# Another issue order and other buffer numbers for a gated linear attention with a mixer behind it, on one core

## The chip, the core and the metric

The kernel runs on one core of one Trainium2 chip. A core has a matrix engine (TensorE, PE in the profile), three engines for elementwise work (VectorE, DVE; ScalarE, ACT; GpSimd, POOL), a fifth that here only issues transfers (SyncE, SP), and DMA engines that move data between memory and the core's buffers and can transpose a block on the way. Each engine runs its own instructions in program order, and waits on semaphores for what the others produce. The metric is the device time of one execution in microseconds. Inputs and output are float32 in memory; the products run in bfloat16 with float32 sums.

## The reference, cut to what matters

Four batches, eight heads, 768 positions, 48 channels a head. First a linear attention whose state decays by its own factor `alpha` for every channel and position; then an MLP mixer over the result, once across the positions and once across the 384 channels.

```
def _attn_ref(q, k, v, alpha):                       # each (4, 8, 768, 48)
    for t in range(S):
        state = alpha[:, :, t, :, None] * state + np.einsum('bhd,bhe->bhde', k[:, :, t], v[:, :, t])
        y[:, :, t] = np.einsum('bhd,bhde->bhe', q[:, :, t], state)

def _moe_ref(x, w_tok1, w_tok2, w_ch1, w_ch2):       # x: (4, 768, 384)
    h = np.maximum(x.transpose(0, 2, 1) @ w_tok1, 0.0) @ w_tok2      # 768 -> 256 -> 768
    u = x + h.transpose(0, 2, 1)
    return u + np.maximum(u @ w_ch1, 0.0) @ w_ch2                    # 384 -> 1536 -> 384
```

## The kernel before

**The attention** goes in 12 chunks of 256 positions, three to a batch; a number at the end of a name is the chunk. A chunk loads alpha, k, q and v (`ld_at`, `ld_kt`, `ld_qt`, `ld_vt`, each 384 KB, all issued by SP). ACT takes logarithms of alpha (`ln`, or `ln1` and `lnP` of products `P` of two neighbours), PE sums them along the positions (`cum`, `cumw` in chunks 0 to 2), ACT makes exponentials of the sums (`E` and `IE`), and `kk` and `qq` multiply k and q with them into pkk and pkq. Both are transposed into tpk and tpq: in chunks 0 to 5 by PE (`trk`, `trq`) with a copy out of the matrix engine's buffer (`evk`, `evq`), in chunks 6 to 11 by a transposing DMA that SP issues (`dk`, `dq`), with a last rearrangement `pq` of q. PE forms the products of q and k inside the chunk (`G0_`, `G1_`), DVE masks them into gtm (`mask0_`, `mask1_`, 128x1024 each). `vb` casts v, `vs0_`, `vs1_`, `ka`, `kb` and `kc` are copies that bring k and v into the form for `K`, the update of the state; `s` and `sa` with `sm` add and scale the state; `ia`, `ib` and `y0_`, `y1_` are the two parts of the output, which `x0_` and `x1_` bring out as the mixer's input.

**The mixer** goes batch by batch. `t1` and `t2` with `ht` between are the mixing across positions, `u` the addition. The transpose of u into ut is done on PE in batch 0 (`up`, `ut`) and by two transposing DMAs in batches 1 to 3 (`ux`). Then come `c1_b_mc_half` (12 column blocks of the channel layer by two halves of the positions, three matmuls of 384 columns each), its relu `rt`, `c2_b_i_q` (four groups of three matmuls for each of six row blocks), the last addition `o` and the store `st`. Weights come in 16 loads `ldw` and 16 casts `cw`. `f...` are matmuls on data that nobody reads, put ahead of a named operation.

**What sets the order.** There is no scheduler left in the file. Every operation is made as an object with its engine's alternatives, its inputs and its buffers, and a table `ORDER` names all of them in one row; the last letter of an entry is the engine (t PE, s ACT, v DVE, g POOL, y SP). They are issued in that order, so the table sets the order on each engine and, where an operation can run on two or three, which. A second table `BUFS` gives each value its buffer or bank: 21 input buffers, 8 banks of the matrix engine, 23 buffers for relu outputs and so on, taken in the order of first use. A third, `GATES`, is empty. `Plan.run` reads them:

```
out = [by[n] for n, _ in order]
for o, (_, e) in zip(out, order):
    o.on, o.gate = ENGINES[e], by.get(gates.get(o.name))
    for v in o.vals:
        if v.buf is None:
            v.buf = next(bufs)
```

One more rule ties engines together: where DVE and POOL (and their operations marked `port`) follow each other in the table, `shared` adds a dependency from the last one of the other engine, so that the two never run such operations at once. The transfers of SP share a few semaphores in turn, so that a transfer is issued when an earlier one that used the same semaphore has landed. Whatever engine issues an operation, it waits for the values that it reads and for the last reader of the buffer that it overwrites. So a load that stands behind a transposition in SP's row waits until that transposition's input is there.

Of the kernel before, what the change touches and what calls it, by code (L numbers as in the profile page):

```python
# [420 lines left out]
ld_vt2y vb2s vs1_2g vs0_2s G1_2t x0_1s K2t t1_0_0_0t t1_0_0_1t ib1t y1_1t ldw_wt11y cw_wt11s ldw_wt21y t1_0_0_2t
t1_0_1_0t t1_0_1_1t ia2t y0_2t t1_0_1_2t sa0_2v sm0_2g ib2t mask1_2v y1_2t x1_1s t1_0_0_3t t1_0_1_3t x0_2s t1_0_0_4t
t1_0_1_4t x1_2s t1_0_1_5t ht_0_1v ld_at4y P4g ldw_wt20y cw_wt20g t1_0_0_5t ht_0_0s f2_t2_0_2t t2_0_2t ln14s u_0_2v
cw_wt21g t2_0_1t u_0_1v t2_0_5t t2_0_3t u_0_3v t2_0_0t r14s ld_at3y ld_kt3y ln13s P3g t2_0_4t lnP4s cum4t lnP3s
up_0_1t ut_0_1s cum3t IE3s u_0_0v up_0_0t u_0_4v u_0_5v up_0_2t ldw_wc12y cw_wc12g ut_0_0v c1_0_4_0t c1_0_5_0t r13s
k0a3g kk3v trk3t ldw_wc10y kb3g cw_wc10s c1_0_0_0t ldw_wc13y cw_wc13s rt_0_4_0v ut_0_2v rt_0_5_0v rt_0_0_0v c1_0_1_0t
ld_qt3y E3s c1_0_1_1t c1_0_5_1t rt_0_1_0v q0r3g qq3v evk3s IE4s ka3v kc3v ldw_wc14y cw_wc14s ldw_wc15y cw_wc15g
rt_0_1_1s c1_0_0_1t rt_0_0_1s c1_0_6_0t trq3t c1_0_7_0t rt_0_6_0s ld_qt4y c1_0_4_1t q0r4g rt_0_7_0v E4s qq4g ldw_wc11y
rt_0_4_1s rt_0_5_1v c1_0_11_0t rt_0_11_0s c1_0_8_0t rt_0_8_0s cw_wc11s ld_vt3y vb3g vs0_3g c1_0_9_0t c1_0_10_1t
rt_0_9_0s evq3v G1_3t mask1_3v G0_3t mask0_3v c1_0_9_1t rt_0_10_1s c1_0_2_1t rt_0_2_1s ld_kt4y k0a4g kk4g vs1_3s  # L430
rt_0_9_1s c1_0_11_1t c1_0_8_1t rt_0_8_1s rt_0_11_1s c1_0_3_0t rt_0_3_0v trq4t evq4s ldw_wc20y ld_at5y ln15s K3t s0_3v
P5g c1_0_2_0t rt_0_2_0v sa1_3v c1_0_10_0t rt_0_10_0v c1_0_3_1t c1_0_7_1t trk4t rt_0_3_1s kb4s rt_0_7_1v evk4v
ldw_wc21y cw_wc21g ldw_wc22y ld_kt5y lnP5s c1_0_6_1t rt_0_6_1v cw_wc20s ld_vt4y ib3t y1_3t x1_3s G0_4t cum5t G1_4t
mask0_4v E5s y0_3t sm1_3g IE5s c2_0_4_0t mask1_4v x0_3v ka4g kc4g k0a5g kk5v c2_0_5_0t c2_0_3_0t c2_0_0_0t ld_qt5y
cw_wc22s c2_0_3_1t r15s q0r5v c2_0_0_1t c2_0_4_1t vb4s vs0_4s vs1_4s ia4t qq5v y0_4t x0_4s K4t sa0_4v trk5t trq5t
c2_0_5_1t ldw_wc23y ldw_wc24y ldw_wc25y cw_wc24v cw_wc23s c2_0_0_2t c2_0_5_2t evq5v sm0_4g sa1_4v sm1_4v c2_0_4_2t
evk5s G1_5t mask1_5v G0_5t cw_wc25s c2_0_5_3t o_0_5v c2_0_3_2t c2_0_3_3t o_0_3v c2_0_4_3t kc5s ld_vt5y vb5g vs0_5s K5t
sa0_5v ld_at6y ib4t y1_4t P6g lnP6s c2_0_0_3t t1_1_0_0t t1_1_0_1t t1_1_1_0t t1_1_1_1t t1_1_1_2t ia5t x1_4s t1_1_1_3t
sm0_5g mask0_5v y0_5t ib5t vs1_5v y1_5t cum6t t1_1_0_2t t1_1_0_3t ln16s x0_5s t1_1_1_4t ld_at8y ld_kt6y P8v lnP8s
t1_1_0_4t x1_5v t1_1_0_5t IE6s t1_1_1_5t ht_1_1s E6s k0a6g kk6g r16s kb6s ka6g ld_qt6y c2_0_2_0t c2_0_2_1t ld_at7y P7g  # L440
ln17s r17s lnP7s o_0_0v ht_1_0v ld_kt7y ld_vt6y o_0_4v t2_1_2t u_1_2v dk6y c2_0_1_0t t2_1_0t u_1_0v t2_1_1t u_1_1v
ux_1_0y t2_1_3t u_1_3v t2_1_5t u_1_5v q0r6g vb6g t2_1_4t u_1_4v cum8t IE8s c2_0_1_1t c2_0_1_2t E8s c2_0_1_3t o_0_1v
cum7t c2_0_2_2t c2_0_2_3t o_0_2v IE7s c1_1_10_0t c1_1_11_0t c1_1_3_0t rt_1_3_0s rt_1_11_0v c1_1_5_0t ln18s rt_1_5_0s
c1_1_8_0t qq6v k0a7g kk7v ux_1_1y c1_1_6_1t E7s rt_1_6_1s vs1_6v rt_1_8_0v c1_1_11_1t c1_1_1_0t c1_1_4_0t rt_1_4_0s
c1_1_2_0t c1_1_0_1t c1_1_10_1t c1_1_3_1t rt_1_10_1s rt_1_3_1s ld_at10y ld_qt7y kc6g q0r7g rt_1_1_0v rt_1_0_1v
c1_1_0_0t c1_1_8_1t c1_1_9_0t rt_1_2_0v rt_1_0_0s rt_1_11_1s r18s qq7g c1_1_7_1t rt_1_10_0v ld_qt8y ld_at9y rt_1_8_1s
c1_1_1_1t rt_1_1_1v c1_1_5_1t rt_1_5_1v dq6y rt_1_7_1v c1_1_4_1t rt_1_4_1v c1_1_6_0t ld_kt8y vs0_6g K6t c2_1_2_0t
s0_6v sa1_6v c1_1_7_0t c2_1_2_1t q0r8g qq8g pq6s G1_6t mask1_6v k0a8g kk8g rt_1_9_0s P10g G0_6t mask0_6v rt_1_6_0s
rt_1_7_0s c1_1_2_1t c1_1_9_1t c2_1_2_2t dq7y dk7y ln19s c2_1_2_3t pq7s o_1_2v G1_7t mask1_7v P9v ka7s kc7g rt_1_2_1s
G0_7t mask0_7v ld_vt7y c2_1_1_0t c2_1_1_1t c2_1_1_2t sm1_6g ld_vt8y vb8g dq8y ib6t c2_1_0_0t y1_6t x1_6v c2_1_0_1t  # L450
c2_1_1_3t o_1_1v vb7s vs0_7s vs1_7s kb7s K7t sa0_7v ln110s c2_1_0_2t rt_1_9_1s sm0_7v sa1_7v dk8y pq8s y0_6t ia7t
y0_7t ld_kt9y c2_1_3_0t c2_1_3_1t G0_8t r110s vs0_8g kc8g G1_8t mask0_8v c2_1_3_2t c2_1_3_3t x0_6s r19s x0_7s lnP9s
o_1_3v cum9t vs1_8s sm1_7g K8t sa0_8v c2_1_0_3t t1_2_1_0t t1_2_1_1t ib7t sm0_8g y1_7t x1_7s t1_2_0_0t ld_kt10y ld_qt9y
ld_at11y k0a10g t1_2_1_2t ia8t mask1_8v y0_8t t1_2_0_1t x0_8s ib8t y1_8t o_1_0v x1_8v t1_2_1_3t ld_vt9y ld_qt10y
t1_2_0_2t t1_2_0_3t t1_2_0_4t t1_2_1_4t t1_2_0_5t P11g ht_2_0s lnP11s E9s t1_2_1_5t ht_2_1v c2_1_5_0t c2_1_5_1t lnP10s
t2_2_4t t2_2_3t q0r9v qq9g t2_2_0t t2_2_5t t2_2_2t ld_kt11y u_2_4v u_2_3v u_2_5v cum11t E11s IE9s t2_2_1t u_2_2v
u_2_1v c2_1_5_2t IE11s c2_1_4_0t q0r10g c2_1_5_3t u_2_0v cum10t IE10s E10s c2_1_4_1t ux_2_1y c2_1_4_2t c2_1_4_3t
c1_2_9_1t k0a9g kk9v ka9v c1_2_7_1t qq10g o_1_4v rt_2_7_1v o_1_5v c1_2_10_1t c1_2_8_1t rt_2_8_1s dq9y pq9g k0a11g
kk10g c1_2_11_1t rt_2_11_1v rt_2_10_1v ln111s c1_2_6_1t rt_2_6_1s ux_2_0y c1_2_1_0t c1_2_10_0t rt_2_10_0s rt_2_9_1v
c1_2_8_0t c1_2_3_0t c1_2_5_1t rt_2_5_1v rt_2_8_0s st_1_0y dk9y kc9s G0_9t mask0_9v G1_9t rt_2_3_0s kk11v mask1_9v  # L460
# [523 lines left out]
```

## Time and profile before

| what | us |
|---|---|
| runs | 161.72, 162.14, 161.7 |
| median of the runs | 161.72 |
| the profiled execution's own time | 162.03 |
| its span, first to last instruction | 160.3 |

The profile is of one execution, on the core's own clock from the first instruction of the span. The difference of 1.7 us between its time and its span lies before and behind. The page gives each engine's busy time, and groups of instructions by source line with their mean duration in nanoseconds; a row of the stages (windows) gives, after the stretch, its length, then the busy time and number of instructions of PE, PE's weight loads (PEld), DVE, ACT, POOL and SP, then the granted clock of PE as a share of full speed, the busy share of the DMA engines and what they moved in GB/s. The chain of waits lists what ended last at each moment, followed back from the last instruction: start, length, engine and line. A row of a timeline is start, length, engine, line, operation, output and inputs, and in square brackets the idle time in front of it and what ended it. A row of the DMA list has the number of issues and the median time from the issue to the landing.

PE is the engine with the most work, 152.1 of 160.3 us. DVE has 115.0, ACT 99.1, POOL 75.9.

### The profile page before, as it was taken

What the parts mean: (1) busy time and instruction counts of PE and PEld (TensorE: products, weight loads), DVE (VectorE), ACT (ScalarE), POOL (GpSimd) and SP (SyncE); (2) the same over time, 40 slices, a digit from 0 to 9 for tenths busy, and PEclk for the clock granted to TensorE, in tenths of its full rate; (3) what the DMA queues carried; (4) which work ended last, traced back from release to release, by engine and by line L of the source; (5) the groups of instructions that cost most, each with busy time, mean ns of one, the idle gap of its engine ahead of it and who ended that gap; (6) DMA issues with size and microseconds to landing.
All of it is one profiled execution on the core that took longest, in us unless ns stands there. A gap on an engine that the chain in (4) does not pass through costs nothing.

```text
span 160.3 us, 3961 instructions
## 1 busy us (share of the span) xinstructions
PE 152.1 (95%) x1555; PEld 96.6 (60%) x1555; DVE 115.0 (72%) x205; ACT 99.1 (62%) x183; POOL 75.9 (47%) x91
## 2 busy tenths in 40 slices
...
GB/s 120 325 325 330 364 338 304 352 313 294 335 210 352 252 305 125 207 252 221 218 216 175 325 309 76 216 236 188 276 149 0 4 76 247 70 98 4 222 195 123
DMA packets 77922, 35.05 MB, mean 219 GB/s; under 512 B 70352, under 2 KB 77136, under 8 KB 77904
## 3 DMA queue, kind: packets, MB, share of 16 engines
...
q8 instruction: 12, 0.20, 0.5%
q14 instruction: 6, 0.05, 0.1%
...
## 4 chain that ended last, share of the span: by engine, by line
PE 75%; ACT 7%; DMA 6%; DVE 6%; issue 3%; POOL 1%; SPq 1%; DVEq 0%; POOLq 0%
PE ps L920 29%; PE ps L925 25%; PE ps L661 9%; PE ps L896 5%; PE ps L901 4%; DMA in<-in_alpha_dram 3%; DMA in<-in_v_dram 3%; PE ps L730 2%; ACT vb L763 2%; DVE u L905 2%; DVE pkq L718 1%; DVE pkk L718 1%; ACT tpq L763 1%; ACT x L763 1%; DVE tmp L859 1%
## 5 line engine op out<-in xcount | busy, mean ns | idle before, releaser
L925 PE MATMUL ps<-wc,rt 128*128 128x384 bf16 (+1 forms) x300 | 53.2, 319 | 0.0
L920 PE MATMUL ps<-ut,wc 128*128 128x384 bf16 x288 | 49.6, 326 | 0.1
L891 ACT ACTIVATE rt<-ps 128x384 bf16<-128x384 f32 x55 | 25.4, 490 | 25.2 <-PE ps L920 20.2
L920 PEld LDWEIGHTS <-wc 128*128 128x128 bf16 x288 | 27.5, 98 | 17.8 <-DMA ut<-u 0.3
L925 PEld LDWEIGHTS <-rt 128*128 128x128 bf16 x300 | 27.4, 97 | 15.8
L893 DVE TENSOR_SCALAR rt<-ps 128x384 bf16<-128x384 f32 x41 | 21.2, 553 | 13.6 <-PE ps L920 13.0
L788 DVE TENSOR_TENSOR gtm<-ps,mk 128x1024 bf16<-128x1024 f32 x24 | 28.7, 1218 | 3.2 <-PE ps L661 2.7
L929 DVE TENSOR_TENSOR rt<-ps,u 128x384 f32<-128x384 f32 (+1 forms) x25 | 13.4, 538 | 9.9 <-PE ps L925 9.6
L862 POOL TENSOR_TENSOR ss<-tmp,E 128x384 bf16<-128x384 f32 x12 | 10.0, 836 | 15.0 <-DVE tmp L859 9.6
L718 POOL TENSOR_TENSOR pkq<-in,E 128x768 bf16<-128x768 f32 x7 | 12.7, 1815 | 6.7 <-DVE pkq L718 3.4
L763 ACT CAST x<-ps 128x384 bf16<-128x384 f32 x17 | 8.1, 477 | 11.8 <-PE ps L661 11.8
L905 DVE TENSOR_TENSOR u<-ps,x 128x384 bf16<-128x384 f32 x24 | 11.7, 551 | 4.4 <-PE ps L901 4.1
L763 ACT CAST vb<-in 64x384 bf16<-64x384 f32 (+1 forms) x19 | 11.6, 612 | 2.7 <-DMA in<-in_v_dram 1.3
L718 DVE TENSOR_TENSOR pkk<-in,in 128x768 bf16<-128x768 f32 x8 | 7.7, 956 | 6.3 <-ACT in L705 4.3
L710 POOL TENSOR_TENSOR in<-in,in 128x384 f32<-128x384 f32 x9 | 9.0, 1002 | 5.1 <-DVE pkq L718 3.8
L764 POOL CAST vb<-in 64x384 bf16<-64x384 f32 (+1 forms) x13 | 8.5, 650 | 5.2 <-DVE ss L862 2.8
L896 PE MATMUL ps<-x,wt 128*128 128x384 bf16 x48 | 10.5, 325 | 0.0
L661 PE MATMUL ps<-rt 128*128 128x512 bf16 (+1 forms) x21 | 8.9, 528 | 1.1 <-DVE rt L547 1.1
L859 DVE TENSOR_TENSOR tmp<-ps,ss 128x384 f32<-128x384 f32 x16 | 8.8, 552 | 0.8 <-PE ps L661 0.4
L901 PE MATMUL ps<-ht,wt 128*128 128x384 bf16 x48 | 8.9, 326 | 0.1
L661 PE MATMUL ps<-tpq,tpk 48*64 48x128 bf16 (+1 forms) x288 | 8.4, 218 | 0.7 <-ACT tpq L763 0.5
L661 PE MATMUL ps<-vb,gtm 128*128 128x48 bf16 x192 | 8.7, 183 | 0.3 <-DVE gtm L788 0.3
...
## 6 DMA issues: line engine op xcount, KB each, us to landing
...
```

Source lines behind the costliest of these rows:

```text
L661: return self.pe.matmul(out, lhsT=lhsT, rhs=rhs, start=start, stop=stop, skip_group_check=True)
L718: self.shared(self.eng[e].tensor_tensor(self.t(dst)[:, :, h0:h1, 0:D], self.t(src)[:, h0:h1].rearrange("p h s d -> p s h d"), bass.AP(tens ...
L763: return self.act.copy(d, s)
L788: self.nc.vector.tensor_tensor(self.t(gtm)[:, hf, :, :], self.pair(gp).rearrange("p a (j t) -> p (a j) t", t=128), bass.AP(tensor=m.tensor ...
L891: self.act.activation(d, s, AF.Relu)
L893: self.nc.vector.tensor_scalar_max(d, s, 0.0)
L896: self.pe.matmul(self.bank(bank)[:, 0:HD], lhsT=self.wt1[:, kc, m * 128 : m * 128 + 128], rhs=self.t(x), start=(kc == 0), stop=(kc == NS - 1))
L901: self.pe.matmul(self.bank(bank)[:, 0:HD], lhsT=self.wt2[:, i // 3, kc, i % 3 * 128 : i % 3 * 128 + 128], rhs=self.t(hts[kc]), start=(kc = ...
L905: self.nc.vector.tensor_tensor(self.t(u)[:, i % 3], self.bank(bank)[:, 0:HD], self.t(x), ALU.add)
L920: self.pe.matmul(self.bank(bank)[:, 0:HD], lhsT=self.wc1[:, kc, mc * 128 : mc * 128 + 128], rhs=self.t(ut)[:, 3 * half : 3 * half + 3, kc, ...
L925: self.pe.matmul(self.bank(bank)[:, 0 : cz - ca], lhsT=self.t(rts[mc][0])[:, i * 128 : i * 128 + 128], rhs=self.wc2[:, mc, ca:cz], start=( ...
L929: self.nc.vector.tensor_tensor(self.o(o, i, ca, cz), self.bank(bank)[:, 0 : cz - ca], self.t(u)[:, i % 3, ca:cz], ALU.add)
```

## The change

Only the two tables are replaced. Every operation stays as it was, the same matmuls, relus, masks, loads and transpositions; 934 entries become 937, since the matmuls on unread data are put ahead of other operations (f8, f1, f2, f4, f1, f2, f4, f1, f2, f2, f1, f1 in place of f12, f2, f2, f1, f1, f3, f1, f2, f2). 144 operations change their engine (relus, copies, casts and products that two or three engines can do, and 11 stores), in both directions: ACT has 199 entries in place of 194, DVE 181 in place of 182, POOL 78 in place of 79, SP 92 in place of 95 (three stores go to ACT). In the shared turn of DVE and POOL, hand-overs from one to the other fall from 31 to 21. `ORDER` is one line longer, so that every line behind it has a number higher by one. The first lines of the diff:

```diff
 ORDER = """
-ld_kt0y ld_at0y ld_at1y ln0s f12_cumw0t f2_cumw0t cumw0t ld_at2y ln1s cumw1t IE0s kk0v f2_trk0t trk0t E0s ld_qt0y qq0v
-trq0t ln2s cumw2t evk0v ka0g kb0v kc0v E1s ld_vt0y vb0s vs1_0v vs0_0v f1_K0t K0t IE1s ld_kt1y kk1v E2s evq0s ld_qt1y
...
+ld_at0y ld_at1y ln0s f8_cumw0t f1_cumw0t cumw0t ln1s cumw1t ld_kt0y IE0s ld_qt0y E0s kk0v qq0v IE1s f2_trk0t trk0t
+evk0v trq0t evq0v f4_G0_0t f1_G0_0t G0_0t mask0_0v ld_qt1y E1s ka0s ld_vt0y vb0s kc0s kb0g qq1g trq1t ld_at2y ln2s
...
```

How rows move is shown at three places.

**The start, on ACT.** `la` are the logarithms of chunks 0, 1 and again 0 for chunk 2 (two buffers), `in` out of `ps` is IE, `E` is E, `vb` the cast of v, `tpq` out of `ps` is evq, `kt` and `pkk` out of `pkk` are the copies ka and kc. The order before:

```order
L655 ACTIVATE la_0_85<-in_1_65 128x16x48
L655 ACTIVATE la_1_86<-in_3_67 128x16x48
L705 ACTIVATE in_2_66<-ps_63 128x768
L701 ACTIVATE E_0_89<-ps_63 128x800
L655 ACTIVATE la_0_85<-in_6_70 128x16x48
L701 ACTIVATE E_1_90<-ps_63 128x800
L763 CAST vb_0_98<-in_1_65 128x768
L705 ACTIVATE in_4_68<-ps_63 128x768
L701 ACTIVATE E_2_91<-ps_63 128x800
L763 COPY tpq_0_105<-ps_63 128x2x512
L705 ACTIVATE in_6_70<-ps_63 128x768
```
And of the change, the same stretch:

```order
L656 ACTIVATE la_0_85<-in_0_64 128x16x48
L656 ACTIVATE la_1_86<-in_2_66 128x16x48
L706 ACTIVATE in_1_65<-ps_63 128x768
L702 ACTIVATE E_0_89<-ps_63 128x800
L706 ACTIVATE in_0_64<-ps_63 128x768
L702 ACTIVATE E_1_90<-ps_63 128x800
L764 COPY kt_0_97<-pkk_0_94 64x8x48
L764 CAST vb_0_98<-in_7_71 128x768
L764 COPY pkk_0_94<-pkk_0_94 64x8x48
L656 ACTIVATE la_0_85<-in_6_70 128x16x48
L764 COPY tpq_1_106<-ps_63 128x2x512
L706 ACTIVATE in_6_70<-ps_63 128x768
```
The logarithm of chunk 2 (the third `la` row) has gone from the fifth place to the tenth, behind ka0, vb0 and kc0 (`kt`, `vb`, `pkk`), two of which DVE or POOL did before; IE1 stands ahead of E1 in the fifth place, where it stood behind vb0; and evq1 is the only evq left in the stretch, since evq0 goes to DVE.

**SP's row from the transposition of batch 1's u on.** `ut<-u` are the two halves ux_1_0 and ux_1_1, `tpk<-pkq` the transpositions of q (dq6, dq7, dq8), `tpk<-pkk` that of k (dk7). Before:

```order
L747 DMA_TRANSPOSE ut_132<-u_130 128x9x128
L600 DMA in_82<-in_alpha_dram 128x8x96
L600 DMA in_77<-in_q_dram 128x8x96
L600 DMA in_70<-in_q_dram 128x8x96
L600 DMA in_73<-in_alpha_dram 128x8x96
L743 DMA_TRANSPOSE tpk_104<-pkq_92 128x8x128
L600 DMA in_67<-in_k_dram 128x8x96
L743 DMA_TRANSPOSE tpk_102<-pkq_93 128x8x128
L743 DMA_TRANSPOSE tpk_101<-pkk_95 128x8x128
L600 DMA in_72<-in_v_dram 128x8x96
L600 DMA in_79<-in_v_dram 128x8x96
L743 DMA_TRANSPOSE tpk_104<-pkq_92 128x8x128
```
And of the change:

```order
L748 DMA_TRANSPOSE ut_132<-u_130 128x9x128
L601 DMA in_72<-in_v_dram 128x8x96
L601 DMA in_74<-in_q_dram 128x8x96
L744 DMA_TRANSPOSE tpk_104<-pkq_92 128x8x128
L601 DMA in_73<-in_q_dram 128x8x96
L601 DMA in_70<-in_k_dram 128x8x96
L601 DMA in_65<-in_v_dram 128x8x96
L744 DMA_TRANSPOSE tpk_102<-pkq_93 128x8x128
L601 DMA in_77<-in_alpha_dram 128x8x96
L744 DMA_TRANSPOSE tpk_101<-pkk_95 128x8x128
```
The load of v of chunk 7, which stood in the tenth place behind dq6, dq7 and dk7, stands in the second directly behind ux_1_1; v of chunk 8 stands ahead of dq7, where it stood behind dk7; the loads of alpha of chunks 10 and 9 have left the place in front of dq6, one for later and one for a place behind dq7.

**DVE's row around chunk 10.** `gtm` are masks (here of chunk 9), `pkk` is kk, `pkq` is qq, `rt` with two operands is a relu, `rt` with `u` the last addition o, `ss` and `tmp` state additions. Before:

```order
L893 TENSOR_SCALAR rt_135<-ps 128x384
L788 TENSOR_TENSOR gtm_108<-ps,mk 128x1024
L718 TENSOR_TENSOR pkk_96<-in_78,in_81 128x16x48
L788 TENSOR_TENSOR gtm_108<-ps,mk 128x1024
L893 TENSOR_SCALAR rt_135<-ps 128x384
L893 TENSOR_SCALAR rt_151<-ps 128x384
L893 TENSOR_SCALAR rt_154<-ps 128x384
L893 TENSOR_SCALAR rt_144<-ps 128x384
L893 TENSOR_SCALAR rt_143<-ps 128x384
L855 TENSOR_TENSOR ss_114<-ps,E_89 128x384
L859 TENSOR_TENSOR tmp_109<-ps,ss_114 128x384
L893 TENSOR_SCALAR rt_134<-ps 128x384
```
And of the change:

```order
L894 TENSOR_SCALAR rt_135<-ps 128x384
L789 TENSOR_TENSOR gtm_108<-ps,mk 128x1024
L894 TENSOR_SCALAR rt_151<-ps 128x384
L789 TENSOR_TENSOR gtm_108<-ps,mk 128x1024
L894 TENSOR_SCALAR rt_154<-ps 128x384
L719 TENSOR_TENSOR pkk_96<-in_84,in_82 128x16x48
L894 TENSOR_SCALAR rt_153<-ps 128x384
L719 TENSOR_TENSOR pkq_93<-in_78,E_90 128x16x48
L894 TENSOR_SCALAR rt_155<-ps 128x384
L856 TENSOR_TENSOR ss_111<-ps,E_89 128x384
L860 TENSOR_TENSOR tmp_109<-ps,ss_111 128x384
L930 TENSOR_TENSOR rt_133<-ps,u_127 128x384
```
Before, kk11 stands between the two masks of chunk 9 and kk10 runs on POOL; now kk10 stands behind the second mask and a relu, with qq11 one relu behind it, and the state additions of chunk 9 (`ss`, `tmp`) behind those. The transposition dk10 on SP waits for kk10, and G0 and G1 of chunk 10 on PE wait for dk10.

127 lines of the change are left out of this document (64 added, 63 removed), and 22 rows, old and new, of the table BUFS.

## The prediction

> **What bounds the kernel now.** I read the page's busy times first, then the busy time by stages, then the chain of waits.
>
> ```profile
> PE 152.1 (95%) x1555; PEld 96.6 (60%) x1555; DVE 115.0 (72%) x205; ACT 99.1 (62%) x183; POOL 75.9 (47%) x91
> ...
> 0.00:30.84 30.84, 26.36 (x302) 15.77 (x303) 22.81 (x54) 24.05 (x37) 16.06 (x29) 1.00 1.04 305
> 30.84:85.00 54.16, 54.16 (x557) 35.21 (x558) 46.02 (x73) 42.20 (x81) 35.18 (x37) 1.00 0.99 256
> 85.00:92.00 7.00, 6.52 (x103) 4.35 (x99) 5.41 (x10) 5.62 (x11) 3.35 (x5) 1.00 1.23 251
> 117.00:157.20 40.20, 40.14 (x348) 25.58 (x346) 21.02 (x39) 10.59 (x21) 1.83 (x3) 1.00 0.31 103
> 157.20:160.40 3.20, 0.00 (x0) 0.00 (x0) 0.34 (x1) 0.00 (x0) 0.00 (x0) 1.00 0.40 146
> ```
>
> The second number of a stage row is PE's busy time. From 30.84 us to 157.2 PE is never idle but for 0.48 us between 85 and 92. A busy row can hide gaps, so I look at the pitch of the matmuls in the chain:
>
> ```profile
> 30.84 1.14 PE ps L920 x6
> 67.32 10.24 PE ps L920 x63
> 133.66 9.80 PE ps L920 x60
> ```
>
> 10.24/63 and 9.80/60 are 163 ns a matmul of 384 columns, early and late. So in this middle PE issues one matmul behind the other, and no order can shorten it except by taking out waits. (The Trainium skill, Perfetto Trace Analysis, section Identifying the Most-Contended Engine, calls matmul busy time a poor measure of headroom and would look at the LDWEIGHTS share; that is 60% here, and by it some 60 us could be won. The equal pitch speaks against it, and the sum goes by the pitch.) The span is then three pieces: the time until the first channel matmul (30.84), PE's work after it with its waits, and a tail of 3.1 us behind the last matmul. An order can change the first, the waits of the second, how much work is done before 30.84, and a little of the third.
>
> **The waits that the old order has.** PE's timeline and the chain around its only idle time:
>
> ```profile
> 87.30 1.14 PE L925 MATMUL ps<-wc,rt 128*128 128x384 bf16 x6
> 88.69 0.64 PE L661 MATMUL ps<-tpq,tpk 48*64 48x128 bf16 x32 [0.25 <-ACT tpq L763]
> 89.26 1.15 PE L925 MATMUL ps<-wc,rt 128*128 128x384 bf16 x6
> 90.64 0.32 PE L661 MATMUL ps<-la,u 128*128 128x384 bf16 x1 [0.23 <-ACT la L652]
> ...
> 78.89 0.04 SPq L743
> 78.98 4.49 DMA in<-in_v_dram
> 83.49 0.84 ACT vb L763
> 88.50 0.52 ACT lf L658
> 90.17 0.43 ACT la L652
> ...
> 77.69 1.24 SPq L743 DMA_TRANSPOSE tpk<-pkk  x1
> 80.35 3.12 SPq L743 DMA_TRANSPOSE tpk<-pkq  x1
> 87.28 1.35 ACT L763 COPY tpq<-tpk 128x1024 bf16<-128x1024 bf16 x1 [0.44 <-DMA tpk<-pkq]
> ```
>
> Six matmuls from 87.30 are through at 87.30 + 6 x 0.163 = 88.28, and G of chunk 8 begins at 88.69: 0.41 late. In the same way 89.26 + 0.98 = 90.24 against 90.64: 0.40 late. The chain says why: v of chunk 7 is asked for at 78.98, behind a transposition on SP, lands 4.49 later, and ACT is pushed back from 83.49 to 90.6 (vb, its halves, pq8, the logs, lnP9). The new order asks for v of chunk 7 directly after the second transposition of batch 1's u, ahead of dq6, and for v of chunk 8 ahead of dq7. **Term a:** both waits go, -0.8. Bounds: 0 (another input of G0_8 or cum9 is as late) and -0.81.
>
> **The start.** PE's, DVE's and ACT's timelines in the first 25 us (start, length, instruction, and in brackets the idle time before it with what ended it):
>
> ```profile
> 6.41 0.65 PE L661 MATMUL ps<-la,u 128*128 128x384 bf16 x3 [0.26 <-ACT la L655]
> 8.34 0.96 DVE L718 TENSOR_TENSOR pkk<-in,in 128x768 bf16<-128x768 f32 x1 [4.27 <-ACT in L705]
> 10.37 0.84 ACT L763 CAST vb<-in 128x768 bf16<-128x768 f32 x1
> 5.52 0.84 ACT L655 ACTIVATE la<-in 128x768 bf16<-128x768 f32 x1 [3.44 <-DMA in<-in_alpha_dram]
> 6.71 0.84 ACT L655 ACTIVATE la<-in 128x768 bf16<-128x768 f32 x1 [0.35 <-DMA in<-in_alpha_dram]
> 7.50 0.81 ACT L705 ACTIVATE in<-ps 128x768 f32<-128x768 f32 x1
> 11.80 0.85 ACT L701 ACTIVATE E<-ps 128x800 f32<-128x800 f32 x1
> 14.72 1.32 ACT L763 COPY tpq<-ps 128x1024 bf16<-128x1024 bf16 x1 [0.20 <-PE ps L730]
> 16.06 1.04 ACT L763 COPY kt<-pkk 64x384 bf16<-64x384 bf16 x2
> 19.62 1.01 ACT L763 COPY tpk<-ps 128x1024 bf16<-128x1024 bf16 x1
> 17.76 0.96 DVE L718 TENSOR_TENSOR pkk<-in,in 128x768 bf16<-128x768 f32 x1
> 19.77 0.55 DVE L859 TENSOR_TENSOR tmp<-ps,ss 128x384 f32<-128x384 f32 x1
> 23.43 1.22 DVE L788 TENSOR_TENSOR gtm<-ps,mk 128x1024 bf16<-128x1024 f32 x1
> 14.39 0.68 DVE L764 COPY tpk<-ps 128x1024 bf16<-128x1024 bf16 x1
> ```
>
> Two loads that follow each other land 6.71 - 5.52 = 1.19 apart. The first two alphas move from places 2 and 3 of SP's queue to 1 and 2, so ln0, ln1 and IE0 come 1.2 us earlier, and k of chunk 0, now third, lands when the second alpha did: kk0 starts near 7.2, not 8.34. But the third alpha falls from place 4 to 7 and lands near 6.7 + 4 x 1.2 = 11.5, and ACT then has in one row vb0 0.84, kc0 0.51, ln2 0.84, evq1 1.32, IE2 0.81, E2 0.85, evk1 1.01 = 6.2, less some 0.1 of overlap each, from vb0's load at 10.4 on: 16.1. Behind it stands G0_1, as late as it was before the change. The lead is kept on DVE alone, which has masked one more G by then. Before, DVE ran without a gap from 17.76 to 24.65 (one kk of 0.96, four masks of 1.22, three additions of 0.55, a little overlapped). Now it has one kk and one mask less, and an evk (0.68) and an x (0.48, L763 on ACT takes as long) more, but the evk waits for kk2, which went to POOL: qq2 and kk2 there are 1.8 each from about 16.05, the transposes end near 20.3, then 0.68 + 0.55 + 1.22 + 0.55 + 1.22 less overlaps is 24.3. Against 24.65 that is 0.3 earlier; two weight casts placed ahead of ht0 and among the t2 take some of it. **Term b:** -0.2; bounds -1.1 (all of the lead kept) and +0.3.
>
> POOL's 1.8 and the rest of the durations by group:
>
> ```profile
> L718 POOL TENSOR_TENSOR pkk<-in,in 128x768 bf16<-128x768 f32 x4 | 7.3, 1821 | 0.2
> tpk<-pkk SPq DMA_TRANSPOSE x6, 3.8
> ut<-u SPq DMA_TRANSPOSE x6, 2.9
> 31.97 0.45 PE ps L730 x8
> 90.93 0.33 PE L661 MATMUL ps<-vb,pkk 128*128 128x96 bf16 x4
> ```
>
> **Term c:** the eight transposes trk3 (0.45) now stand ahead of the first channel matmul, and cum4 stands behind it (a cum takes 90.93 - 90.64 = 0.29): -0.15. Fill matmuls lie before the first channel matmul in both orders and are inside term b.
>
> **Term d, the tail.** In the old order the last two additions stand apart; now o_3_4 (0.55, as a u or tmp row) ends about when the last half matmul does and o_3_0h0 follows at once: +0.05, bounds 0 and +0.2 (two stores closer together).
>
> **Term e, new waits.** The tightest place is chunk 10. DVE has, from the end of G0_9 on, mask0_9 1.22, a relu, mask1_9 1.22, a relu, kk10 0.96; with 0.55 a relu and 0.09 of overlap each that is 4.05, and 0.45 for G0_9 itself and the hand-over. Then dk10 is issued and must land before G1_10. PE has between G0_9 and G1_10 fourteen groups of three matmuls (0.49), K9 and G0_9 itself (0.33 each): 7.5. So dk10 has 7.5 - 4.5 = 3.0 us. The transposes of u, which have no load in front of them, take 2.9; those of pkk 3.8 in the median, with loads in front. Ahead of dk10 no load is issued for some 6 us, so I take the 2.9 and the wait at 0.2; bounds 0 and 0.8. Besides, G0_5 waits for evq5: trq5 (0.45 and its end) and 1.32 on ACT against 0.45 + 3 x 0.49 of PE, 0.1 to 0.2. **Term e:** +0.4, bounds 0 and +1.9.
>
> **Sum** against the profiled execution: 160.3 - 0.8 - 0.2 - 0.15 + 0.05 + 0.4 = 159.6, 0.7 less. That execution took 162.03, 1.7 outside its span; the median of the runs is 161.72, so 161.72 - 0.7 = 161.0; as the tight places can only add, I say 161.1.
>
> **Rivals.**
> 1. **The wait moves.** Term a is won, but dk10 takes the 3.8 of the median row against the 3.0 that it has: PE waits 0.8 at G1_10 in place of 0.2, 161.1 + 0.6 = 161.7, no change. For it: the median of six such transpositions; against: no load in front of this one.
> 2. **Slower: dk10 behind traffic.** dq8 was issued at 80.35 and its reader on ACT, idle until then, started at 87.28, so a transposition has taken up to 6.9 here. If dk10 takes 4.9 or more, PE stands 1.9 at G1_10 in place of 0.2, and nothing behind it gives that back, since K10, sa, sm, K11, the masks, t1_3 and the last mixer follow one from the other: 161.1 + 1.7 = 162.8. It decides from a landing 4.2 us after the issue on. For it: two of three kinds of transposition have medians of 3.8 and more; against: these lay behind two or three loads, dk10 lies behind another transposition alone.
> 3. **Head of the line on ACT.** vb7 now stands ahead of four relus. v of chunk 7 is issued 0.5 us before the batch's first channel matmul, and c1_1_3_0, eleven groups (5.4) later, needs the bank that the first of them empties; 5.4 + 0.5 - 0.84 - 0.6 leaves the load 4.4. The old one took 4.49, behind a transposition; at 5.5 PE loses 1.1: 162.2. Little chance alone; it is counted with rival 2.
> 4. **Better than forecast.** The new waits stay hidden and half of the start's lead is kept: 161.1 - 0.4 - 0.4 = 160.3.
> 5. **A slow start.** cumw0 would come at 5.2 in place of 6.41, with 8 + 1 fills before it in place of 12 + 2. The 0.65 that three matmuls take at 6.41 is the pace of the rows at 90 us (0.32 for one, 0.16 for each further one); at half that pace, an assumption, cumw0 and cumw1 take 1 us more, of which vb0's wait for its load hides 0.5: 161.6. The granted clock is 1.00 in every stage shown above, and no row here shows a slow start. (The Trainium skill, TensorE: Matmul & The Clock Gate, section Part 1: The HAM clock gate, says that the pace of the array follows its activity over a window of some 3.4 us that runs freely, so fewer fills could leave it slow in some runs; no run here shows it.)
>
> **How the numbers follow.** The forecast has 0.46, rival 1 0.16, rivals 2 and 3 0.15, rival 4 0.16, rival 5 0.07. What a measurement of this kernel can tell from no change is about 0.3%, 0.49 us: faster is below 161.23, slower above 162.21. The forecast's own range is 160.6 to 161.6, of which a fifth lies in the band; so faster is 0.36 + 0.16 = 0.52; same is 0.10 + 0.12 (rival 1) + 0.04 (rival 5) = 0.26; slower 0.15 + 0.04 + 0.03 = 0.22. The range goes from rival 4 to between rivals 3 and 2: 160.2 to 162.5.
>
> **What would show it.** Right: no idle time of PE between 85 and 92, the first channel matmul at 30.6, the last matmul's end near 156.3, DVE's last mask of chunk 2 ending near 24.3. Wrong: idle time of PE at the G of chunk 10 or 11, put down to the DMA of tpk or to ACT; an ACT wait for in_v_dram near 68 to 72 with PE waiting for rt behind it; a first channel matmul later than 30.84; or waits of 0.4 on PE at places that this text does not name, which would mean that the tightness lies in the banks and not in the transfers.

## The result, and the profile after

| | kernel before | new kernel |
|---|---|---|
| median, first comparison | 162.16 (22 runs) | 163.38 (22 runs) |
| ratio, 95% interval | | 1.0074 (1.0052 to 1.0095) |
| median, second comparison | 161.68 (35 runs) | 163.46 (12 runs) |
| ratio, 95% interval | | 1.0101 (1.0079 to 1.0123) |
| span of the profiled execution | 160.3 | 161.9 |
| first channel matmul | 30.84 | 30.53 |
| end of the last matmul | 157.14 | 158.55 |

The new kernel is slower by 0.7 to 1.0%, 1.2 to 1.8 us; the forecast was 161.1, faster, with a range of 160.2 to 162.5, and both medians lie above that range. The forecast started from a median of 161.72 in three executions; in the first comparison the kernel before has 162.16, so against a change of -0.6 the runs have +1.2. The ratios and their intervals leave out the few executions in which the chip was slower as a whole, and are not the quotients of the medians shown. The stages of the new kernel first, columns as in the prediction (length, then busy time and instructions of PE, weight loads, DVE, ACT and POOL, granted clock, DMA share, GB/s):

```profile
30.53:85.00 54.47, 53.83 (x553) 34.38 (x554) 43.25 (x69) 44.70 (x84) 39.89 (x39) 1.00 0.98 254
85.00:119.00 34.00, 32.41 (x356) 20.57 (x354) 28.17 (x47) 22.25 (x44) 15.31 (x18) 1.00 0.99 221
119.00:158.55 39.55, 39.55 (x347) 25.37 (x345) 20.30 (x37) 10.00 (x21) 2.72 (x4) 1.00 0.29 96
```

PE stands idle for 0.64 us before 85 and for 1.59 between 85 and 119; before, it was 0.48 between 85 and 92 and none in the stage ahead of that. The line of the page that gives the chain of waits by engine, of the kernel before and of the new one:

```profile
PE 75%; ACT 7%; DMA 6%; DVE 6%; issue 3%; POOL 1%; SPq 1%; DVEq 0%; POOLq 0%
```

```profile
PE 64%; DMA 15%; POOL 6%; DVE 5%; ACT 4%; issue 3%; SPq 2%; POOLq 0%; DVEq 0%
```

What PE lost in the chain went to the DMA engines (9 points) and to POOL (5). PE's timeline of the new kernel at the only three places after 31 us where the view shows a wait:

```profile
82.67 0.64 PE L662 MATMUL ps<-tpq,tpk 48*64 48x128 bf16 x32 [0.64 <-DMA tpk<-pkk]
108.58 0.98 PE L662 MATMUL ps<-tpq,tpk 48*64 48x128 bf16 x32 [0.91 <-ACT tpq L764]
117.38 0.64 PE L662 MATMUL ps<-tpq,tpk 48*64 48x128 bf16 x32 [0.55 <-DMA tpk<-pkk]
```

These are G of chunks 7, 9 and 10, and the chain (start, length) says what they waited for:

```profile
77.29 5.33 DMA tpk<-pkk
...
101.05 6.11 DMA tpk<-pkq
107.17 0.02 issue
107.19 1.34 ACT tpq L764
...
113.83 3.50 DMA tpk<-pkk
```

All three are transposing DMAs: dk7, dq9 (with pq9 behind it on ACT) and dk10. SP's timeline shows what was issued just ahead of the first two:

```profile
76.67 0.58 SPq L601 DMA_DIRECT2D in<-in_alpha_dram  x1
77.29 2.12 SPq L744 DMA_TRANSPOSE tpk<-pkk  x1
...
99.74 0.58 SPq L601 DMA_DIRECT2D in<-in_q_dram  x1
100.37 0.57 SPq L643 DMA_DIRECT2D out_dram<-rt  x1
101.05 2.02 SPq L744 DMA_TRANSPOSE tpk<-pkq  x1
```

Ahead of dk7 stands the load of alpha of chunk 9; ahead of dq9 the load of q of chunk 10 and a store. In the kernel before, SP's timeline has only a transposition directly ahead of each:

```profile
75.83 1.75 SPq L743 DMA_TRANSPOSE tpk<-pkq  x1
77.69 1.24 SPq L743 DMA_TRANSPOSE tpk<-pkk  x1
...
97.80 1.29 SPq L747 DMA_TRANSPOSE ut<-u  x1
99.19 1.25 SPq L743 DMA_TRANSPOSE tpk<-pkq  x1
```

There dk7 landed 3.10 us after its issue and dq9 2.73.

**Where the 1.5 us between the two spans went.** For each group of matmuls of one operation I take the time from its start to the start of the next, less the median of its kind in the kernel before; so a group's usual pitch counts as nothing. Between the first channel matmul and the end, the surplus is 1.53 us before and 3.40 after. The new kernel has 0.71 at G0_7, 1.20 at G1_9 and G0_9, 0.62 at G1_10, in sum 2.53. The kernel before has 0.32 at G0_8, 0.40 at cum9, 0.12 at G1_10, in sum 0.84. So the difference is made of: start -0.31, work that now lies ahead of the first channel matmul -0.16 (sum of the medians 124.37 and 124.21), old waits -0.84, new waits +2.53, tail +0.12 (3.18 and 3.30), and 0.18 spread over places of less than 0.1 each. The sum is +1.52; the spans, 160.32 and 161.85, differ by 1.53.

### The profile page after: what moved, and what is told of

The parts are those of the page before. It is cut to its first block, busy times and chain, and to the rows that moved or that the text cites. A ratio compares the mean times of both kernels' runs of the same rounds, so it can differ in the third digit from the quotient of the medians.

```text
span 161.9 us, 3944 instructions
## 1 busy us (share of the span) xinstructions
PE 152.8 (94%) x1559; PEld 95.7 (59%) x1559; DVE 115.5 (71%) x204; ACT 101.2 (63%) x185; POOL 77.4 (48%) x90
## 3 DMA queue, kind: packets, MB, share of 16 engines
q10 hardware_dynamic: 2160, 2.85, 4.8%
## 4 chain that ended last, share of the span: by engine, by line
PE 64%; DMA 15%; POOL 6%; DVE 5%; ACT 4%; issue 3%; SPq 2%; POOLq 0%; DVEq 0%
PE ps L926 25%; PE ps L921 17%; PE ps L662 10%; DMA tpk<-pkk 5%; PE ps L897 5%; PE ps L902 4%; DMA tpk<-pkq 4%; DMA in<-in_q_dram 3%; DMA in<-in_alpha_dram 3%; PE ps L731 2%; POOL pkq L719 2%; DVE pkk L719 1%; POOL pkk L719 1%; SPq L601 1%; POOL in L715 1%
## 5 line engine op out<-in xcount | busy, mean ns | idle before, releaser
L926 PE MATMUL ps<-wc,rt 128*128 128x384 bf16 (+1 forms) x300 | 51.9, 320 | 0.0
L892 ACT ACTIVATE rt<-ps 128x384 bf16<-128x384 f32 x48 | 21.8, 489 | 18.7 <-PE ps L921 9.6
L894 DVE TENSOR_SCALAR rt<-ps 128x384 bf16<-128x384 f32 x48 | 24.9, 552 | 11.6 <-PE ps L921 11.5
L764 ACT CAST vb<-in 64x384 bf16<-64x384 f32 (+1 forms) x23 | 14.0, 608 | 2.7 <-DMA in<-in_v_dram 1.5
L719 POOL TENSOR_TENSOR pkq<-in,E 128x768 bf16<-128x768 f32 x8 | 14.5, 1817 | 0.4
L719 POOL TENSOR_TENSOR pkk<-in,in 128x768 bf16<-128x768 f32 x6 | 10.9, 1816 | 5.0 <-ACT in L698 2.5
L765 POOL CAST vb<-in 64x384 bf16<-64x384 f32 (+1 forms) x10 | 6.3, 630 | 9.6 <-DVE pkk L719 5.3
L647 POOL TENSOR_TENSOR in<-in 128x384 f32<-128x384 f32 x9 | 8.9, 999 | 3.1 <-DVE in L711 3.0
L662 PEld LDWEIGHTS <-tpk 48*64 48x64 bf16 (+1 forms) x288 | 5.8, 102 | 7.5 <-DMA tpk<-pkk 2.6
L715 POOL TENSOR_TENSOR in<-in,lf 128x384 f32<-128x384 f32 x8 | 7.9, 997 | 3.3 <-ACT lf L659 2.7
```

The lines of the kernel that those rows point to most:

```text
L662: return self.pe.matmul(out, lhsT=lhsT, rhs=rhs, start=start, stop=stop, skip_group_check=True)
L719: self.shared(self.eng[e].tensor_tensor(self.t(dst)[:, :, h0:h1, 0:D], self.t(src)[:, h0:h1].rearrange("p h s d -> p s h d"), bass.AP(tens ...
L764: return self.act.copy(d, s)
L892: self.act.activation(d, s, AF.Relu)
L894: self.nc.vector.tensor_scalar_max(d, s, 0.0)
L926: self.pe.matmul(self.bank(bank)[:, 0 : cz - ca], lhsT=self.t(rts[mc][0])[:, i * 128 : i * 128 + 128], rhs=self.wc2[:, mc, ca:cz], start=( ...
```

## The experiments

Theories at the start. **Q**: a transposition lands only after the loads asked for just ahead of it, and the new order puts such loads ahead of dk7 and dq9. **L**: the transpositions are late because of late inputs or traffic at that moment, whatever stands ahead. **M**: waits only move, so one taken away comes back at the next place. The pieces of the table that move are shown; the buffers stay each operation's own, and the table of their numbers is written anew in the order of first use.

**late_at9**, one load moved.

```diff
-y1_6t kb7g ld_at9y dk7y c1_1_5_1t
+y1_6t kb7g dk7y c1_1_5_1t
...
-dk8y kc8s ld_at11y
+dk8y ld_at9y kc8s ld_at11y
```

> The new kernel with one load moved: alpha of chunk 9 is asked for behind dk8 instead of directly ahead of dk7. Theory Q (a transposition lands only after the loads asked for just ahead of it on SP): dk7 lands 2.7 to 3.2 us after its issue in place of 5.33, the wait of 0.71 at G0_7 goes, 163.4 - 0.7 = 162.7. Rival L (the transpositions are late because of the traffic or of late inputs at that moment, whatever stands ahead): dk7 still takes 5 us, 163.4. Rival M (a wait taken away comes back at the next one): the wait at G0_7 goes, that at G1_9 grows by 0.7, 163.4.

dk7 landed 2.96 us after its issue, and the wait at G0_7 went. PE's waits in the new kernel and in this one (us in total, times, longest):

```profile
PE ps L662 <- DMA tpk<-pkk: 1.2, 2, 0.6
PE ps L662 <- ACT tpq L764: 0.9, 1, 0.9
```

```profile
PE ps L662 <- ACT tpq L764: 0.9, 1, 0.9
PE ps L662 <- DMA tpk<-pkk: 0.6, 1, 0.6
```

One of the two DMA waits is gone, the others have not grown: against L and, here, against M. The median was 163.04, where 162.7 was expected. Its ratio to the kernel before, 1.0086 (1.0056 to 1.0116), lies between the new kernel's two ratios, so the trace shows this gain and the times do not; the run new_again below shows why a part of this wait is not always there.

**late_qt10_st02**, the load of q of chunk 10 and the store moved behind dk9, with q0r10, which reads that q.

```diff
-rt_2_9_1s ld_qt10y c1_2_3_0t
+rt_2_9_1s c1_2_3_0t
...
-q0r11g q0r10g c1_2_4_1t
+q0r11g c1_2_4_1t
...
-rt_2_7_1s st_0_2y dq9y pq9s rt_2_0_0s rt_2_4_1s kb9s dk9y
+rt_2_7_1s dq9y pq9s rt_2_0_0s rt_2_4_1s kb9s dk9y ld_qt10y q0r10g st_0_2y
```

> The new kernel with the load of q of chunk 10 and the store st_0_2 moved from ahead of dq9 to behind dk9 (and q0r10, which reads that q, behind them in the table). Theory Q: dq9 lands some 2.8 us after its issue in place of 6.12, the waits of 1.2 at G1_9 and G0_9 go, 163.4 - 1.2 = 162.2; G0_7 still waits 0.7. Rival L: dq9 still takes 5 to 6 us, 163.4. Rival M: the wait at G1_9 goes and that at G1_10 grows by as much, 163.4.

dq9 took 4.21 in place of 6.11 (2.8 was expected), and the waits at G1_9 and G0_9 went. But G1_10 now waits 1.06 in place of 0.62, though dk10 lands fast, as the chain shows:

```profile
111.02 2.73 DMA tpk<-pkq
114.26 2.71 DMA tpk<-pkk
```

q of chunk 10 landed at 108.03 in place of 104.14, so q0r10, qq10, k0a10 and kk10 followed later on POOL and DVE, and dk10 was issued at 114.26. Median 163.1, 1.0084 (1.0057 to 1.0112): what a wait gives, the next row takes, a part of M.

**all_three**, both moves, and mask1_9 behind kk10 on DVE.

```diff
-c1_2_9_0t rt_2_9_0v mask1_9v c1_2_5_0t
+c1_2_9_0t rt_2_9_0v c1_2_5_0t
...
-k0a10g kk10v c2_2_1_0t
+k0a10g kk10v mask1_9v c2_2_1_0t
```

> The new kernel with both moves, and with mask1_9 on DVE behind kk10, so that dk10 is issued 1.0 us earlier. Theory Q: the three waits of 2.5 us in all go, 160.9, which is 0.8% below the kernel before. Rival L: 163.4, or 162.8 with only dk10 earlier. Rival M: 162.5 to 163.4, with waits at places that had none.

165.5, 1.0225 (1.0183 to 1.0267): far off. DVE's timeline:

```profile
110.58 0.56 DVE L894 TENSOR_SCALAR rt<-ps 128x384 bf16<-128x384 f32 x1 [0.84 <-PE ps L921]
112.74 0.96 DVE L719 TENSOR_TENSOR pkk<-in,in 128x768 bf16<-128x768 f32 x1 [1.60 <-POOL in L711]
113.61 1.22 DVE L789 TENSOR_TENSOR gtm<-ps,mk 128x1024 bf16<-128x1024 f32 x1
```

kk10 waits 1.60 for POOL's k0a10, and everything behind it on DVE waits too: the mask, and the relus whose banks PE needs. PE then stood 2.56 us longer than usual before K9 and 0.3 to 0.5 at each of four groups after it. The third part of this edit, the mask behind kk10, cost more than the two moves won: two_moves below, without it, takes 162.76. In the trace of late_qt10_st02, too, kk10 waits 1.30 for k0a10, but there no mask stands behind it.

**before_v_early**, the kernel before with the early loads of v that term a is about.

```diff
-c1_1_8_0t qq6v k0a7g kk7v ux_1_1y c1_1_6_1t
+c1_1_8_0t qq6v k0a7g kk7v ux_1_1y ld_vt7y c1_1_6_1t
...
-c2_1_2_2t dq7y dk7y
+c2_1_2_2t ld_vt8y dq7y dk7y
```

> The kernel before with only v of chunk 7 asked for directly behind ux_1_1 and v of chunk 8 ahead of dq7. If term a of the prediction is right by itself: the waits of 0.32 and 0.40 at G0_8 and cum9 go, 162.2 - 0.7 = 161.5. Theory Q adds that dq6 and dq7, now with one load more ahead, land 1 to 2 us later; if their readers feel it, PE waits at G1_6 or G1_7 and the gain is lost: 162.2. Rival: something else at G0_8 is as late, 162.2 without any new wait.

162.93, 1.0065 (1.004 to 1.0091): slower. G0_8 and cum9 do not wait, but G1_7 does (PE's timeline), and the chain has both transpositions of q ahead of it:

```profile
83.73 0.47 PE L661 MATMUL ps<-tpq,tpk 48*64 48x128 bf16 x20 [1.04 <-ACT tpq L763]
```

```profile
73.18 9.13 DMA tpk<-pkq x2
82.31 0.02 issue
82.33 1.35 ACT tpq L763
```

dq7 took 5.36 behind v of chunk 8, where it had taken 4.06. The move that was to win term a pays more than it wins, by the same price that the new kernel pays at dk7.

**new_again**, the new kernel unchanged.

> The new kernel once more, unchanged, beside the next three on the same chip. Both theories: the ratio to the kernel before as first measured, 1.005 to 1.010, and in its trace the three waits at G0_7, G1_9 with G0_9, and G1_10.

1.0101 (1.0079 to 1.0123), with all three waits: 0.20 at G0_7, 1.29 at G1_9 and G0_9, 0.60 at G1_10. Its first channel matmul came at 31.05, 0.52 later than in the first trace (term b below says why), and dk7 landed at 82.66 against 82.63: a late start is taken out of the wait at G0_7, whose end the transfers set.

**two_moves**, ld_at9 behind dk8, and ld_qt10 and st_0_2 behind dk9, as above, without the change on DVE.

> The new kernel with ld_at9 behind dk8, and with ld_qt10 and st_0_2 behind dk9; DVE's order as in the new kernel. Theory Q: dk7 and dq9 land 2.7 to 3.7 us after their issue, the waits at G0_7 (0.7) and G1_9 with G0_9 (1.2) go, G1_10 keeps the 1.06 that it had in the run with the second move alone (0.4 more than in the new kernel): the new kernel's time less 1.5. Rival M: the waits that remain grow to the sum of the old ones, the new kernel's time less 0.3 at most.

162.76, 1.0053 (1.0025 to 1.008), 0.7 below new_again, which was measured beside it, where 1.5 was expected; the two intervals just touch. G0_7, G1_9 and G0_9 do not wait; G1_10 waits 1.05 and two relus of DVE, behind kk10, come late (PE's timeline):

```profile
113.93 1.15 PE L926 MATMUL ps<-wc,rt 128*128 128x384 bf16 x6 [0.24 <-DVE rt L894]
115.26 0.34 PE L926 MATMUL ps<-wc,rt 128*128 128x384 bf16 x1 [0.18 <-DVE rt L894]
116.22 0.64 PE L662 MATMUL ps<-tpq,tpk 48*64 48x128 bf16 x32 [0.62 <-DMA tpk<-pkk]
```

So 1.9 of waits were taken away and some 0.9 came back in chunk 10's row of loads, products and transposition.

**loads_apart**, all of it mended: k and q of chunk 10 in SP's idle time, the move of ld_at9, and vb11 (now on POOL), vs1_11 and vs0_11 later to fit.

```diff
-sm0_8v vb9v ld_vt11y
+sm0_8v vb9v ld_kt10y
...
-t1_2_0_5t ld_qt11y c2_1_5_0t
+t1_2_0_5t ld_qt10y c2_1_5_0t
...
-IE11s kk11v c1_2_1_1t
+IE11s kk11v k0a10g c1_2_1_1t
...
-c1_2_3_0t vs1_9v c1_2_7_1t
+c1_2_3_0t vs1_9v kk10v c1_2_7_1t
...
-kb9s dk9y c1_2_7_0t
+kb9s dk9y ld_qt11y st_0_2y c1_2_7_0t
...
-kc9g c1_2_4_0t rt_2_4_0s st_0_1y ld_kt10y k0a10g kk10v c2_2_1_0t
+kc9g q0r11g c1_2_4_0t rt_2_4_0s st_0_1y dk10y dq10y ld_vt10y ld_vt11y c2_2_1_0t
```

> The new kernel with ld_at9 behind dk8, with k and q of chunk 10 asked for in SP's idle time ahead of ux_2_1 (in the places of v and q of chunk 11, which go behind dk9 and dq10), with dk10 issued ahead of dq10, and with k0a10, kk10, q0r11, vb11 and its copies moved to fit on POOL and DVE. Theory Q: dk7, dq9, dk10 land within 3.5 us, and none of the three waits is left; PE's matmuls lie as close as its work allows but for 0.3: the new kernel's time less 2.2, or some 0.7 below the kernel before. If ux_2_1, now behind k and q of chunk 10, lands later than 100, PE waits there for up to 1.5 and the gain shrinks to 0.7. Rival M: not below the kernel before.

No wait is left at any G; dk7, dq9 and dk10 took 3.01, 3.59 and 2.72. The median is 161.74, 0.9984 (0.9963 to 1.0004) of the kernel before and 1.7 below new_again: with the three transpositions free of loads, the loss is gone. The edit also changes the engine of vb11 and moves kk10 and other copies, which were not tried by themselves. The 0.7 below the kernel before did not come.

**before_dq8_clear**, the kernel before with v of chunk 7 in the place of alpha of chunk 10, and that alpha behind dk8.

```diff
-rt_1_3_1s ld_at10y ld_qt7y kc6g
+rt_1_3_1s ld_vt7y ld_qt7y kc6g
...
-dk8y pq8s
+dk8y ld_at10y pq8s
```

> The kernel before with v of chunk 7 in the place of alpha of chunk 10 on SP, and that alpha behind dk8 (its readers P10, ln110, r110 later). So dq6 and dq7 have as many loads ahead as before, and dq8 has one where it had two. Theory Q says that the old waits at G0_8 and cum9 came from dq8, 6.85 us from issue to landing behind v of chunks 7 and 8, not from ACT being pushed back by vb7: dq8 now lands 4.5 us or less after its issue, both waits (0.32 and 0.40) go and none comes in their place: 0.7 below the kernel before. Rival (the prediction's own reading, by vb7 alone): vb7 runs 1.3 us earlier and the waits go too, but dq8 still lands late. Rival M: a wait of 0.5 or more at another G or cum.

No wait at G0_8 or cum9, none new, a span of 159.7; and yet 161.9, 1.0001 (0.9969 to 1.0034). And dq8 took 4.78, where 4.5 or less was expected. A gain that the trace shows and the median does not suggests that most executions of the kernel before do not have that loss; the next two runs look at this.

**before_again** and **before_third**, the kernel before unchanged.

> The kernel before once more, unchanged, for a second trace of it. If term a of the prediction is as large as the first trace showed, G0_8 and cum9 wait 0.32 and 0.40 again, and dq8 lands 6 to 7 us after its issue; if the first execution was unlucky there, less. The first channel matmul of batch 0 came at 30.84, 31.54 and 30.74 in three executions with the same instructions up to there: a fourth value between.

> The kernel before, unchanged, a third trace. In the first, G0_8 and cum9 waited 0.32 and 0.40 and dq8 took 6.85 us; in the second there was no such wait and dq8 took 4.82. Most likely as the second: dq8 4.8 to 5.0, no wait at G0_8 or cum9. If they are there again, the gain that term a counted on is real in about half of the executions.

PE's timeline of the first of them at G0_8 (88.53) and cum9 (90.09), with nothing in brackets, so no wait:

```profile
88.53 0.64 PE L661 MATMUL ps<-tpq,tpk 48*64 48x128 bf16 x32
89.11 1.15 PE L925 MATMUL ps<-wc,rt 128*128 128x384 bf16 x6
90.09 0.33 PE L661 MATMUL ps<-la,u 128*128 128x384 bf16 x1
```

dq8 took 4.82 there and 5.07 in the third trace, which has no such wait either. The three runs below leave that stretch as it is, and have none. So one execution in six had the waits of term a, the one that was shown before the change. With dq8 at 4.82 and 5.07 in the unchanged kernel, the 4.78 of before_dq8_clear is no gain of its edit, and that run decides nothing between theory Q and the prediction's reading. The time of the third run, 162.93, comes mostly from its start: its first channel matmul stood at 32.07.

**loads_by_act**, the new kernel with the three transfers issued by ACT.

```diff
-c1_1_8_0t rt_1_8_0s
+c1_1_8_0t ld_at9s rt_1_8_0s
...
-kb7g ld_at9y dk7y
+kb7g dk7y
...
-ln111s kk9g
+ln111s ld_qt10s kk9g
...
-E10s IE10s c2_1_5_3t
+E10s IE10s st_0_2s c2_1_5_3t
...
-rt_2_9_1s ld_qt10y c1_2_3_0t
+rt_2_9_1s c1_2_3_0t
...
-rt_2_7_1s st_0_2y dq9y
+rt_2_7_1s dq9y
```

> The new kernel with the three transfers that stand ahead of dk7 and dq9 (alpha of chunk 9, q of chunk 10, st_0_2) issued by ACT at about the same times, so that they lie in ACT's queue and no longer in SP's. Theory Q, strict (a transposition waits for what its own queue holds): dk7 and dq9 land 2.7 to 3.6 us after their issue, the waits at G0_7 and at G1_9 with G0_9 go, the new kernel's time less 1.5. Rival E (what counts is what the 16 DMA engines have in hand, from whatever queue): dk7 still takes 4.5 us or more, dq9 too, and the time stays within 0.5 of the new kernel's.

Both halves came out, each for one theory. The load went out from ACT at 76.48 (ACT's timeline, and the view of the transposition's line in that moment):

```profile
76.48 0.43 ACTq L601 DMA_DIRECT2D in<-in_alpha_dram  x1
```

```profile
L744 SPq DMA_TRANSPOSE tpk<-pkk x1: 1312/1312/1312, 76.8 to 76.8; - x1
...
DMA to landing us min/median/max: 5.3/5.3/5.3
```

dk7 took 5.25 although SP's row holds nothing ahead of it: theory Q in its strict form falls, and what fits is **E**: what the DMA engines have in hand counts, whatever queue it came from. Why a load delays a transposition so is not shown. The time fell all the same, to 161.97, 1.0011 (0.9995 to 1.0027): dk7 was issued 0.45 earlier, since SP no longer spends 0.58 on the load, and landed at 82.09, just before G0_7; and q of chunk 10 left at 94.75 in place of 99.74 and landed before dq9 was issued, so dq9 (3.61) says nothing about the queue. Of the three waits only that at G1_10 is left, 0.61.

**before_load_ahead**, **before_load_act** and **before_store_ahead**: the kernel before, where dq9 is clear, with one transfer put ahead of it; a load by SP, the same load by ACT, a store by SP.

```diff
-rt_2_8_1s dq9y
+rt_2_8_1s ld_vt10y dq9y
...
-c1_2_0_1t ld_vt10y c1_2_0_0t
+c1_2_0_1t c1_2_0_0t
```

```diff
-IE11s c2_1_4_0t
+IE11s ld_vt10s c2_1_4_0t
...
-c1_2_0_1t ld_vt10y c1_2_0_0t
+c1_2_0_1t c1_2_0_0t
```

```diff
-rt_2_8_1s dq9y
+rt_2_8_1s st_1_0y dq9y
...
-rt_2_8_0s st_1_0y dk9y
+rt_2_8_0s dk9y
```

> The kernel before with v of chunk 10 asked for directly ahead of dq9, which has nothing ahead of it there and lands after 2.73. The price of one load ahead, by itself: loads land some 4.3 us after their issue and a transposition 0.9 to 1.7 after the load ahead of it, so theory Q expects 4.3 + 1.3 - 0.6 = 5.0 us for dq9, and later landings for ux_2_0 and dk9 behind it. Rival L: 2.7 to 3.3, as the DMA engines are otherwise idle there.

> The kernel before with v of chunk 10 asked for by ACT, about a microsecond ahead of dq9 on SP. Before, dq9 has nothing ahead of it and lands after 2.73 and 2.77; with that load ahead in SP's own row it took 4.56. Theory Q, strict (only the own queue counts): 2.7 to 3.0. Rival E (what the DMA engines have in hand counts, from whatever queue): 4 to 5.5, and PE waits at c1_2_1_0 again.

> The kernel before with the store st_1_0 directly ahead of dq9 on SP in place of behind ux_2_0. A store of 192 KB lands 1.5 to 2.2 us after its issue when it is alone. By both theories dq9 should land some 0.8 to 1.3 us after the store, so it takes 2.7 to 3.4 us: a store ahead is cheap, a load ahead is not. If it takes 4.5 or more, the count of transfers matters and not their kind.

By SP, the landing of dq9 in the view of its line, and in PE's timeline the wait that followed at c1_2_1_0, which needs ux_2_0, issued behind dq9:

```profile
DMA to landing us min/median/max: 4.6/4.6/4.6
```

```profile
105.46 0.82 PE L920 MATMUL ps<-ut,wc 128*128 128x384 bf16 x4 [1.23 <-DMA ut<-u]
```

By ACT, the issue of the load, and in PE's timeline the wait, now at c1_2_9_1, the first that needs ux_2_1, and not at c1_2_1_0 as expected:

```profile
97.04 0.44 ACTq L600 DMA_DIRECT2D in<-in_v_dram  x1
```

```profile
102.21 0.66 PE L920 MATMUL ps<-ut,wc 128*128 128x384 bf16 x3 [1.66 <-DMA ut<-u]
```

The load went out in the same moment as ux_2_1 (97.05), which took 5.12 in place of 2.83 to 2.85, and dq9 behind it 4.55. With the store ahead, dq9 took 2.72, as without it, and PE waited nowhere new. So here a load ahead costs a transposition 1.8 to 2.3 us from either queue, this store nothing. (A store also moves half of a load's bytes, 192 KB against 384, so kind and size are not told apart. Stores of that size with no other transfer in flight took 1.84 to 2.69 us in the traces, not the 1.5 to 2.2 of the expectation.) Of the two transfers ahead of dq9 in the new kernel it was then the load of q that mattered, though the store was not moved alone there. The times, of single executions, were 163.42, 163.09 and 161.34 beside 161.22 to 162.96 of the kernel before.

**loads_apart_tail**, loads_apart with the tail of the kernel before.

```diff
-c2_3_0h1_2t c2_3_0h0_1t rt_3_9_0v
+c2_3_0h1_2t rt_3_9_0v
...
-c2_3_4_3t o_3_4v
+c2_3_4_3t c2_3_0h0_1t o_3_4v
```

> The run loads_apart with one group more of the last half row block behind the last group of c2_3_4, so that o_3_4 and the last addition lie apart as in the kernel before. Expected: as loads_apart, no wait over 0.2 at a G, and the tail 3.2 in place of 3.35 us; 0.1 below loads_apart, 0.2 to 0.4 below the kernel before. Rival: the tail is set by the last store's landing alone, and nothing changes.

161.38, 0.9972 (0.9952 to 0.9992): the one version whose interval lies below the kernel before, by 0.3%. It overlaps the interval of loads_apart, so the times do not show what the tail alone is worth. From the last matmul's end to the end of the span it is 3.14 us, where loads_apart has 3.30. The stage of the new kernel with the largest waits, in this run:

```profile
85.00:119.00 34.00, 34.00 (x377) 21.65 (x376) 30.00 (x49) 21.51 (x44) 15.84 (x18) 1.00 0.94 230
```

PE had 1.59 us of idle time there in the new kernel and has none now.

## Why the prediction was wrong

**Term e, the new waits, is the step that failed.** It said +0.4 with bounds 0 and +1.9, from two places; the new kernel's traces have 2.53 and 2.09. At G1_10 it was right in kind and near in size: 0.62 against 0.2, inside its 0 to 0.8; dk10 landed after 3.50, not 2.9. At G0_5 there is no wait (0.1 and less). But the list was short. G0_7 behind dk7 and G1_9 behind dq9, 1.9 of the 2.5 us, are not in it, although the order shown ahead of the prediction has a load of alpha directly above the transposition of k of chunk 7. The prediction had the price in its own rows, 3.12 issued and 6.9 in all for dq8 behind two loads, 2.9 for a transposition with none in front, and used it for dk10 alone. What was to be done was to go down SP's row of the new order and price every transposition by the loads ahead of it.

**Term a was mis-sized.** The profiled pair has 0.72 of the 0.8 that it forecast, but that is luck of one execution: the waits were there in one trace of six, and before_again, before_third and before_dq8_clear put its worth for the median near nothing. Its reason was wrong too. The text had the chain run from v of chunk 7 over ACT's backlog to G0_8. The last row of that same fence says that pq8 found ACT idle for 0.44 and waited for dq8, which lay behind the loads of v of chunks 7 and 8. Why dq8 took 6.85 that once and 4.79 to 5.07 in the five others, behind the same two loads, stays open. And the move has the price that before_v_early shows: v of chunk 8 ahead of dq7 cost 1.04 at G1_7. In the new order dq7 is issued 3.1 us after the load of v of chunk 8 and lands in time (3.94); there it is dk7, behind alpha of chunk 9, that pays.

**Term b, the start**: -0.31 in the two profiled executions, -0.2 forecast. Over all traces the first channel matmul stands at 30.74 to 32.07 with the old start (eight values, median 30.92) and at 30.51 to 31.13 with the new one (nine values, median 30.93). So the middle did not move, and the 0.31 is luck of the pair too. The slow start of rival 5, with a chance of 0.07, is there in most traces of the new order. PE's timeline at the first matmuls of cumw0, in the new kernel's profiled execution and in new_again:

```profile
5.14 0.65 PE L662 MATMUL ps<-la,u 128*128 128x384 bf16 x3 [0.33 <-ACT la L656]
```

```profile
5.18 1.12 PE L662 MATMUL ps<-la,u 128*128 128x384 bf16 x3
```

The same three matmuls take 1.12 us in place of 0.65, although the profile gives the granted clock as 1.00. In seven of the nine traces all of cumw0 takes 1.23 to 1.69 us in place of 1.04 to 1.05, and their first channel matmul comes at 30.63 to 31.13; the two without it are those at 30.51 and 30.53. In all eight of the old order, which has more matmuls on unread data ahead of it and starts it at least 1.1 us later, cumw0 takes 1.04 to 1.05. No run changes these matmuls alone, so that their number is the cause is not shown.

**Term c**, -0.15: the medians of the groups' pitches add up to 0.16 less. **Term d**, +0.05 with bounds 0 and +0.2: +0.12, and loads_apart_tail took it back.

**The rivals.** Rival 2, slower by a transposition behind traffic, has the right mechanism at the wrong place: dk10 alone was to cost 1.7, and dk7 with dq9 cost 1.9. Its argument against itself, that dk10 has no load in front, was true of dk10 but not of dk7 and dq9. Rival 3 did not come: no relu behind vb7 kept PE waiting. The prediction named what would show it wrong, idle time of PE at a G put down to the DMA of tpk; that is what is there, and at chunks 7 and 9 as well.

The Trainium skill (DMA: Bandwidth & Descriptors, section Issuing engines are not separate DMA queues) says that transfers issued by different engines run on the same 16 DMA engines and interleave, so that another issuer saves only its own time of issue. The runs agree: 5.25 and 5.12 us with the load in ACT's queue, and what loads_by_act won at dk7 was the 0.45 of issue.
